# Other PSUM buffers and a new order for the first batch of an RWKV6 and mixer kernel, and a later place for one range flag

## The chip, the cores and the metric

The kernel runs on one core of a Trainium2 chip. The metric is the device time of one execution in microseconds (us). Of the kernel before there are three runs: 542.96, 543.42 and 543.53 us, with a median of 543.42 us.

A core has five engines that take their instructions in order, each from a queue of its own. TensorE (PE in the profile) multiplies matrices and writes the products to PSUM. VectorE (DVE) and ScalarE (ACT) do elementwise work and read PSUM. SyncE (SP) issues the transfers here, and GpSimd (POOL) has next to nothing to do. PSUM is held in banks of 512 float32 values on each of 128 partitions.

## The reference

There are two parts. The first is a linear attention with a decaying state, for 4 batches, 8 heads, 768 tokens and heads of 48:

```python
for t in range(S):
    cur = np.einsum('bhd,bhe->bhde', u[None] * kt, vt)
    y[:, :, t] = np.einsum('bhd,bhde->bhe', rt, state + cur)
    state = wt[:, :, :, None] * state + np.einsum('bhd,bhe->bhde', kt, vt)
```

The second takes x, which is y with heads and head sizes side by side (4 x 768 x 384), and mixes first over tokens, then over channels:

```python
h = np.maximum(xt @ w_tok1, 0.0) @ w_tok2      # xt: x with tokens last; 768 -> 256 -> 768
u = x + h.transpose(0, 2, 1)
h2 = np.maximum(u @ w_ch1, 0.0) @ w_ch2        # 384 -> 1536 -> 384
return (u + h2).astype(np.float32)
```

The four weights arrive as 64-bit floats. The kernel converts them to float32 itself.

## The kernel before, in words

**Attention by units.** A batch has 768 tokens. A unit is 256 of them, so a batch has three units and there are twelve in all (0 to 11). Within a unit the tokens form four chunks of 64. The loop over tokens of the reference becomes products over chunks, with the decays put into queries and keys. `unit(i)` returns the steps of unit i as functions:

- `ends` (L368) and `begins` (L376) are the running products of the decays (scans on VectorE), `keys` (L373) and `queries` (L379) multiply them into k and r.
- `tokens` (L281) transposes the keys on TensorE into two PSUM banks of the tag "m", and `copied` (L282) copies the two halves to SBUF on ScalarE.
- `carry` (L298) forms the products of keys and values per chunk, the state product `kv_ps`. `update` (L442, L444) adds the chunk's product to the scaled state on VectorE, and `scaled` (L434) scales the new state for the next chunk on ScalarE. So the two alternate: add, scale, add, scale.
- `own_gram` and `gram` (L251) are the products of keys and queries inside a chunk, the first with u. `own_put` (L391) and `mask` (L263, later L421) put them into the matrix `at` on VectorE.
- `before` (L313) multiplies the queries with the states into the PSUM tile of y, `after` (L334) adds the product of `at` and the values. Between them stands `seen` (L322 or L325), a small copy on ScalarE of y's last columns, called the view below. `taken` (L340) copies y to x in three parts.
- `ranges` (L360) are two passes on ScalarE over the decays, each leaving a flag of whether they are in range: `ranges[0]` the lower, `ranges[1]` the upper. The flags are summed near the end.

**PSUM in the first batch.** Three pools share it: `ps_a` with one buffer of two banks, `ps_g` with two buffers of two banks (tag "gram"), `ps_m` with two buffers of one bank (tag "m"). In units 0 to 2 the state product takes two banks of `ps_m`, which the transposed keys use also. y takes `ps_a` in units 0 and 1, and a buffer of `ps_g` in unit 2. After the first batch `ps_g` and `ps_m` make way for one pool of six single banks. From then on the state product takes `ps_a`, and grams, y and everything else single banks.

**Weights and mixing.** The weights are converted in pieces of 128 x 1024 values (`convert`). A piece is loaded, then has steps on VectorE and ScalarE in turn: exponent (L203), power of two (ScalarE, L206), mantissa (L209), sum (L215), signs (ScalarE, L212), product (L218, L221). Two raw buffers, `spare` and `scratch`, take turns; the next load into one waits for the conversion that reads it. The mixing of a batch runs a batch behind its attention: token mixing `hidden` (L515) and `back` (L522, with the add L524), transposes `turn` (L530), channel mixing `up` (L538, with L540 on ScalarE) and the second channel product, plain (L609) or in a form with seven products of quarters (L627, its first VectorE steps L637 and L668).

**Order.** For TensorE, VectorE and ScalarE `strict` fixes the order of issue as written: each instruction is issued after the one before it on its engine. The first batch is one list written out by hand (L718 to L726). In later batches `woven` merges the list of attention steps (`steps`, L687) with the list of mixing pieces by the weights that stand beside each entry, so that an entry's weight shifts what follows it. SyncE's transfers are not in that order; a scheduler places them.

Of the kernel before, what the change touches and what calls it, by code (L numbers as in the profile page):

```python
# [10 lines left out]
f32 = mybir.dt.float32  # L11
# [10 lines left out]
T = 64  # L22
# [40 lines left out]
def rwkv6_then_mixer(  # L63
# [46 lines left out]
    def bank(name):  # L110
        return ps_m.tile([128, 512], f32, name=name, tag="m")
# [175 lines left out]
            f()  # L287
        return kT

    def outer(kT, vt, half, apart=False):  # L290

        both = None if apart else ps_a.tile([128, 2, 512], f32, name="kv_ps", tag="a")
        kv = [bank("kv_ps") if apart else both[:, j] for j in range(2)]
        for c in range(UC):
            for a in range(A):
                for j, q in ((0, 0), (1, 1), (0, 1), (1, 0)):
                    if 2 * (half * UC + c) + j < 2 * C - 1:
                        pe.matmul(kv[j][ts(q, P), ds((c * A + a) * D, D)], kT[ts(j, T), c, a, ts(q, P)],  # L298
                                  vt[ts(j, T), c, ts(2 * a + q, D)], start=True, stop=True)
        return kv  # L300

    def across(r_, before, half, where=None):

        where = where or (ps_g and (ps_a, "a"))
        both = where and where[0].tile([128, 2, 512], f32, name="y_ps", tag=where[1])
        y = [both[:, q] for q in range(2)] if where else [bank("y_ps") for q in range(2)]
        begun = set()
        for c in range(UC):
            for a in range(A):
                for q, j in ((0, 0), (1, 0), (1, 1), (0, 1)):  # L310
                    g = 2 * (half * UC + c) + j
                    if g > 0:
                        pe.matmul(y[q][put(q, j), ds((c * A + a) * D, D)],  # L313
                                  r_[q * P:q * P + D, ds((c * A + a) * 128 + j * T, T)],
                                  before[g][q * P:q * P + D, a, :], start=(q, j) not in begun, stop=False,
                                  skip_group_check=True)
                        begun.add((q, j))

        def see():
            seen = apool.tile([128, 2], f32, name="seen")  # L320
            if where:
                act.copy(seen, both[:, :, X * D - 1])  # L322
            else:
                for q in range(2):
                    act.copy(seen[:, q:q + 1], y[q][:, X * D - 1:X * D])  # L325

        return y, see
# [14 lines left out]
    def unit(i):  # L342
# [78 lines left out]
                dve.tensor_mul(at[:, q], g, over_heads(strictly, g.shape[1]))  # L421

        def carry():
            L["kv"] = outer(L.pop("kT"), vs[i], half, apart=bt == 0)
# [11 lines left out]
        def update(c, j):  # L436
            g = 2 * (half * UC + c) + j
            if g < 2 * C - 1:
                new = state[bt, g + 1] = apool.tile([128, A, D], f32, name="state", bufs=3)
                got = L["kv"][j][:ROWS, ds(c * A * D, A * D)].rearrange("p (a e) -> p a e", a=A)  # L440
                if g == 0:
                    dve.tensor_copy(new[:ROWS], got)  # L442
                else:
                    dve.tensor_add(new[:ROWS], L["before"][g][:ROWS], got)  # L444

        def before():
            if half == 0:
                xs[bt] = xpool.tile([128, C, DM], f32, name="x")
            L["y"], L["see"] = across(r_, L["before"], half, (ps_g, "gram") if i == UB - 1 else None)

        def seen():
            L["see"]()
# [250 lines left out]

    hiddens, turned, ups, downs = mixing_of(0)
# [85 lines left out]
    def by_halves(b):  # L790
# [18 lines left out]
        for half in range(UB):  # L809
# [25 lines left out]
            for c in range(UC):  # L835
                for j in range(2):
                    g = 2 * (half * UC + c) + j
                    if g < 2 * C - 1:
                        new = states[g + 1] = apool.tile([128, A, D], f32, name="before", bufs=5)
                        got = kv[j][:ROWS, ds(c * A * D, A * D)].rearrange("p (a e) -> p a e", a=A)  # L840
# [54 lines left out]
```

## Time and profile before

The figures are of one profiled execution.

| what | value |
|---|---|
| median of the runs | 543.42 us |
| the profiled execution | 546.1 us |
| its span, first to last instruction | 544.3 us |
| mean granted TensorE clock | 0.971 |
| TensorE busy | 509.1 us, 94% |
| VectorE busy | 336.0 us, 62% |
| ScalarE busy | 212.6 us, 39% |

By stage (TensorE busy of the stage, and the clock granted in it):

| us from the start | TensorE busy | clock |
|---|---|---|
| 0 to 15 | 6.33 | 1.00 |
| 15 to 30 | 9.57 | 0.66 |
| 30 to 45 | 9.85 | 0.67 |
| 45 to 60 | 14.14 | 0.88 |
| 60 to 75 | 12.57 | 1.00 |
| 75 to 90 | 14.05 | 1.00 |
| 90 to 110 | 16.97 | 1.00 |
| 110 to 180 | 67.81 | 0.95 |
| 180 to 260 | 79.48 | 1.00 |
| 260 to 340 | 80.00 | 1.00 |
| 340 to 390 | 49.48 | 1.00 |
| 390 to 545 | 148.90 | 1.00 |

In the timeline a row gives the start, the length, the engine, the line, the operation, output <- inputs, the shape and the number of instructions. In brackets stand the idle time before it and what ended that. A wait is written as who waited <- for what: microseconds in total, times, longest. The matmuls of float32 appear as two records each. In the 40 slices of the span a digit is the busy share in tenths, or for PEclk the granted clock in tenths of full speed. Idle time of an engine that is not on the path that sets the end costs nothing.

### The profile page before, as it was taken

How to read it: one execution, taken by the hardware profiler on the slowest of the kernel's cores; microseconds unless marked ns; L12 is line 12 of the kernel's file. 1: busy time of each engine (PE TensorE's matmuls, PEld its weight loads, DVE VectorE, ACT ScalarE, POOL GpSimd, SP SyncE). 2: the span in 40 equal slices, each digit the busy share in tenths (PEclk: the TensorE clock that was granted, in tenths of full speed). 3: DMA queues.
4: the chain of work that ended last, by engine and by line, in shares of the span. 5: the costliest groups of instructions: out<-in, count | busy, mean ns of one | idle time of the engine just before them, and what ended most of it. 6: DMA issues, size and time to landing. Idle time of an engine off the chain costs nothing.

```text
span 544.3 us, 12657 instructions
## 1 busy us (share of the span) xinstructions
PE 509.1 (94%) x5542; PEld 439.9 (81%) x5542; DVE 336.0 (62%) x516; ACT 212.6 (39%) x534; POOL 1.3 (0%) x10
## 2 busy tenths in 40 slices
PE   3659979799899999999999999999999999999996
PEld 3548568676798967898998967898898977999996
DVE  7975999688672755175382655277294625775653
ACT  3856695753234323423324333423514313541400
POOL 0000000000000000000000000000000000000000
PEclk9677999989899999999999999999999999999999
DMA  8855747632321313104113112002000000000000
GB/s 310 327 147 161 251 136 238 208 107 62 97 88 53 108 55 117 40 31 145 41 60 107 51 59 98 30 4 88 1 27 5 2 30 1 1 1 31 1 32 32
DMA packets 20942, 46.01 MB, mean 85 GB/s; under 512 B 2128, under 2 KB 13008, under 8 KB 20880
## 3 DMA queue, kind: packets, MB, share of 16 engines
q1 hardware_dynamic: 20736, 45.14, 25.1%
q8 instruction: 45, 0.74, 0.6%
q14 instruction: 17, 0.14, 0.1%
q10 hardware_dynamic: 144, 0.00, 0.0%
HBM read 40.41 MB, written 4.72 MB: 83 GB/s over the span
## 4 chain that ended last, share of the span: by engine, by line
PE 79%; DVE 11%; ACT 4%; issue 3%; DMA 1%; DVEq 0%; ACTq 0%
PE q_ps L627 27%; PE z_ps L538 22%; PE z_ps L570 6%; PE h_ps L515 5%; PE h_ps L522 4%; PE h_ps L609 3%; PE y_ps L334 3%; PE gram L251 2%; PE kv_ps L298 2%; PE y_ps L313 2%; PE k_ps L281 2%; DVE to_end L368 1%; ACT scratch L212 1%; PE xT_ps L530 1%; DVE scratch L218 1%
## 5 line engine op out<-in xcount | busy, mean ns | idle before, releaser
L538 PE MATMUL z_ps<-xT,wch 128*128 128x256 f32 x648 | 148.9, 385 | 1.0 <-DVE wch L221 1.0
L538 PEld LDWEIGHTS z_ps<-xT,wch 128*128 128x128 f32 x648 | 121.8, 192 | 18.1 <-DVE wch L221 1.4
L627 PE MATMUL q_ps<-wch,z 128*128 128x192 f32 x492 | 87.0, 328 | 0.0
L627 PEld LDWEIGHTS q_ps<-wch,z 128*128 128x128 f32 x492 | 80.4, 190 | 1.3 <-DVE z L669 0.3
L540 ACT ACTIVATE z<-z_ps 128x256 f32<-128x256 f32 x108 | 40.7, 382 | 83.7 <-PE z_ps L538 83.1
L627 PE MATMUL q_ps<-scratch,z 128*128 128x192 f32 x324 | 58.2, 334 | 2.2 <-DVE z L668 2.2
L434 ACT ACTIVATE before<-state,to_end 112x48 f32<-112x48 f32 x176 | 44.2, 323 | 34.4 <-DVE state L444 31.7
L627 PEld LDWEIGHTS q_ps<-scratch,z 128*128 128x128 f32 x324 | 54.6, 195 | 2.7 <-DVE z L668 2.5
L444 DVE TENSOR_TENSOR state<-before,kv_ps 112x192 f32<-112x192 f32 x40 | 14.0, 350 | 44.8 <-ACT before L434 31.4
L522 PE MATMUL h_ps<-h,wtok 128*128 128x384 f32 x96 | 35.2, 492 | 0.6 <-ACT h L517 0.6
L637 DVE TENSOR_TENSOR o<-x,z 128x192 f32<-128x192 f32 x8 | 2.9, 358 | 50.9 <-ACT z L636 46.4
L515 PE MATMUL h_ps<-x,wtok 128*128 128x384 f32 x96 | 32.6, 495 | 0.0
L524 DVE TENSOR_TENSOR x<-x,h_ps 128x384 f32<-128x384 f32 x24 | 13.3, 552 | 27.4 <-PE h_ps L522 27.2
L368 DVE TENSOR_TENSOR_SCAN to_end<-w,starts 112x1041 f32<-112x1041 f32 (+1 forms) x13 | 28.1, 2160 | 2.1 <-DMA w<-in_w_dram 1.7
L376 DVE TENSOR_TENSOR_SCAN w<-w,starts 112x1041 f32<-112x1041 f32 x12 | 27.8, 2320 | 0.0
L515 PEld LDWEIGHTS h_ps<-x,wtok 128*128 128x128 f32 x96 | 18.3, 194 | 11.8 <-issue 0.5
L360 ACT ACTIVATE junk<-to_end,least 112x1041 uint8<-112x1041 f32 x12 | 13.9, 1162 | 28.3 <-DVE to_end L368 28.3
L522 PEld LDWEIGHTS h_ps<-h,wtok 128*128 128x128 f32 x96 | 16.6, 190 | 10.1 <-ACT h L517 2.8
L340 ACT COPY x<-y_ps 64x384 f32<-64x384 f32 (+1 forms) x36 | 17.1, 476 | 18.1 <-PE y_ps L334 17.7
L281 PE MATMUL k_ps<-ident,rk 128*128 128x128 f32 x96 | 15.4, 311 | 6.2 <-issue 4.4
L334 PEld LDWEIGHTS y_ps<-vt,at 64*64 64x64 f32 x768 | 14.5, 148 | 7.3 <-ACT seen L325 4.6
L334 PE MATMUL y_ps<-vt,at 64*64 64x48 f32 x768 | 16.0, 234 | 4.6 <-ACT seen L325 3.3
(140 smaller groups left out, 672.8 us busy)
## 6 DMA issues: line engine op xcount, KB each, us to landing
rk<-in_rk_dram SPq DMA_DIRECT2D x36, 192.0 KB, 3.6
near<-in_near_dram SPq DMA_DIRECT2D x8, 768.0 KB, 4.3
w<-in_w_dram SPq DMA_DIRECT2D x11, 520.5 KB, 3.3
spare<-in_w_ch_dram SPq DMA_DIRECT2D x10, 512.0 KB, 4.5
vt<-in_v_dram SPq DMA_DIRECT2D x12, 384.0 KB, 4.2
out_dram<-o SPq DMA_DIRECT2D x24, 192.0 KB, 1.9
scratch<-in_w_ch_dram SPq DMA_DIRECT2D x8, 512.0 KB, 4.2
rk<-in_rk_dram SPq DMA_DIRECT2D x6, 512.0 KB, 8.6
```

Of the source, the lines that this page charges most:

```text
L281: pe.transpose(both[c][:, a, :], k_[:, ts(c * A + a, 128)], ident)
L334: pe.matmul(y[q][put(q, j), ts(ca, D)], at[ts(j, T), q, ca, :], vt[ts(j, T), c, ts(2 * a + q, D)], start=False, stop=ca == 0, skip_group_c ...
L340: return [lambda: act.copy(x[:, 0], got[0])] + [lambda n=n: act.copy(x[ts(n, P), 1], got[1][ts(1 - n, P)]) for n in range(2)]
L368: dve.tensor_tensor_scan(to, of, start, 0.0, op0=ALU.mult, op1=ALU.add)
L376: dve.tensor_tensor_scan(w_[:ROWS], w_[:ROWS], starts[:ROWS], 0.0, op0=ALU.mult, op1=ALU.add)
L434: act.mul(t[:ROWS, a], state[bt, g][:ROWS, a], by_last(c, j)[:, a:a + 1])
L515: pe.matmul(sums[i], wtok1[:, c, ts(i, 128)], x_of()[:, c, :], start=(c == 0), stop=(c == C - 1))
L522: pe.matmul(ps, wtok2[:, i, ts(c, 128)], h1[:, i, :], start=(i == 0), stop=(i == DTOK // 128 - 1))
L538: pe.matmul(ps, wch1[:, m, ts(jt, 128)], xT[:, m, ts(s, SEG)], start=(m == 0), stop=(m == DM // 128 - 1))
L540: act.activation(zs[s][:, jt, :], ps, AF.Relu)
L570: pe.matmul(ps[:, q], lefts[r][:, ts(q, 128)], of[r], start=first and q == 0, stop=end and q == JB - 1, skip_group_check=True)
L627: pe.matmul(ps, a[:, j, :], b[:, j, :], start=(j == 0), stop=(j == HJ - 1))
```

## The change

There are three edits.

1. In the first batch the state product takes `ps_a`, the buffer that only it uses from now on, and y takes a buffer of the tag "gram" in all three units. The transposed keys and the first mixing products have the two banks of `ps_m` to themselves. `outer` loses its argument `apart`, and `across` its argument `where`.
2. The hand-written order of the first batch is set anew, to match. Unit 1's `own_put` stands ahead of its `carry` and `gram`; unit 2's `keys` and `tokens` stand after the first update of unit 1, with `own_gram` and `carry` later; unit 2's `own_put` and `gram` stand after unit 1's `after`, and only two instead of four of the `hidden` products precede unit 2's y.
3. In units 3 to 11 `ranges[1]` moves from ahead of the last update to the place between `seen` and `after`, and its weight in the weaving is 1.5 instead of 0.4. Since the list of a batch is woven by its total weight, other pieces shift by a place or two too.

```diff
-    def outer(kT, vt, half, apart=False):
-        both = None if apart else ps_a.tile([128, 2, 512], f32, name="kv_ps", tag="a")
-        kv = [bank("kv_ps") if apart else both[:, j] for j in range(2)]
+    def outer(kT, vt, half):
+        kv = ps_a.tile([128, 2, 512], f32, name="kv_ps", tag="a")
...
-    def across(r_, before, half, where=None):
-        where = where or (ps_g and (ps_a, "a"))
-        both = where and where[0].tile([128, 2, 512], f32, name="y_ps", tag=where[1])
-        y = [both[:, q] for q in range(2)] if where else [bank("y_ps") for q in range(2)]
+    def across(r_, before, half):
+        both = ps_g and ps_g.tile([128, 2, 512], f32, name="y_ps", tag="gram")
+        y = [both[:, q] for q in range(2)] if ps_g else [bank("y_ps") for q in range(2)]
...
-            L["y"], L["see"] = across(r_, L["before"], half, (ps_g, "gram") if i == UB - 1 else None)
+            L["y"], L["see"] = across(r_, L["before"], half)
...
-                *([(1.3, e["sums_put"])] if by_tokens else []), (0.4, e["ranges"][1]), (0.7, up[3]),
-                (0.1, lambda: load_w(i + 2)), (1.0, e["before"]), (0.1, e["seen"]), (1.0, e["after"]), *some(e["taken"], 0.3),
+                *([(1.3, e["sums_put"])] if by_tokens else []), (0.7, up[3]),
+                (0.1, lambda: load_w(i + 2)), (1.0, e["before"]), (0.1, e["seen"]), (1.5, e["ranges"][1]), (1.0, e["after"]), *some(e["taken"], 0.3),
...
-           e1["keys"], e0["after"], *e2["own_u"], e1["tokens"], *e1["copied"], e1["queries"], e1["carry"], *e0["taken"], lambda: load_v(2),
-           e1["gram"], e2["ends"], e2["keys"], s1[0], t1[1], e2["tokens"], e1["own_put"], e2["own_gram"], s1[1], t1[2], *e2["copied"],
-           e2["begins"], e2["carry"], s1[2], t1[3], e1["mask"], s1[3], t2[0], e1["before"], e2["queries"], e2["gram"], s2[0], t2[1], e1["seen"],
-           e1["after"], x1, m1, s2[1], t2[2], e1["taken"][0], *h[:4], e2["own_put"], s2[2], t2[3], e1["taken"][1], p1, e2["mask"], e1["taken"][2],
-           s2[3], e2["before"], e2["seen"], add1, g1, put1, to_ch[0][0], e2["after"], *h[4:8], x2, m2, *e2["taken"], p2, add2, g2, *h[8:], put2,
+           e1["keys"], e0["after"], *e2["own_u"], e1["tokens"], *e1["copied"], e1["queries"], e1["own_put"], e1["carry"], *e0["taken"],
+           lambda: load_v(2), e1["gram"], e2["ends"], s1[0], t1[1], e2["keys"], e2["tokens"], s1[1], t1[2], e2["own_gram"], *e2["copied"],
+           e2["begins"], s1[2], t1[3], e1["mask"], s1[3], t2[0], e2["carry"], e1["before"], e2["queries"], s2[0], t2[1], e1["seen"],
+           e1["after"], e2["own_put"], e2["gram"], s2[1], t2[2], x1, e1["taken"][0], m1, *h[:2], s2[2], t2[3], e1["taken"][1], p1, e2["mask"],
+           e1["taken"][2], s2[3], e2["before"], e2["seen"], add1, g1, put1, to_ch[0][0], e2["after"], *h[2:8], x2, m2, *e2["taken"], p2,
+           add2, g2, *h[8:], put2,
```

Here e0, e1, e2 are the units 0 to 2, s1 and t1 the updates and scalings of unit 1, h the `hidden` products, and x, m, p, add, g, put with a number the steps of that weight conversion: exponent, mantissa, power, sum, signs, product.

More of the change, by code (lines that the diff above doesn't have):

```diff
@@ L297, in outer @@
                     if 2 * (half * UC + c) + j < 2 * C - 1:
-                        pe.matmul(kv[j][ts(q, P), ds((c * A + a) * D, D)], kT[ts(j, T), c, a, ts(q, P)],
+                        pe.matmul(kv[ts(q, P), j, ds((c * A + a) * D, D)], kT[ts(j, T), c, a, ts(q, P)],
                                   vt[ts(j, T), c, ts(2 * a + q, D)], start=True, stop=True)
         return kv
-    def across(r_, before, half, where=None):
-        where = where or (ps_g and (ps_a, "a"))
-        both = where and where[0].tile([128, 2, 512], f32, name="y_ps", tag=where[1])
-        y = [both[:, q] for q in range(2)] if where else [bank("y_ps") for q in range(2)]
+    def across(r_, before, half):
+        both = ps_g and ps_g.tile([128, 2, 512], f32, name="y_ps", tag="gram")
+        y = [both[:, q] for q in range(2)] if ps_g else [bank("y_ps") for q in range(2)]
         begun = set()
@@ L320, in see @@
             seen = apool.tile([128, 2], f32, name="seen")
-            if where:
+            if both is not None:
                 act.copy(seen, both[:, :, X * D - 1])
@@ L423, in carry @@
         def carry():
-            L["kv"] = outer(L.pop("kT"), vs[i], half, apart=bt == 0)
+            L["kv"] = outer(L.pop("kT"), vs[i], half)
         def by_last(c, j):
@@ L439, in update @@
                 new = state[bt, g + 1] = apool.tile([128, A, D], f32, name="state", bufs=3)
-                got = L["kv"][j][:ROWS, ds(c * A * D, A * D)].rearrange("p (a e) -> p a e", a=A)
+                got = L["kv"][:ROWS, j, ds(c * A * D, A * D)].rearrange("p (a e) -> p a e", a=A)
                 if g == 0:
@@ L839, in by_halves @@
                         new = states[g + 1] = apool.tile([128, A, D], f32, name="before", bufs=5)
-                        got = kv[j][:ROWS, ds(c * A * D, A * D)].rearrange("p (a e) -> p a e", a=A)
+                        got = kv[:ROWS, j, ds(c * A * D, A * D)].rearrange("p (a e) -> p a e", a=A)
                         if g == 0:
```

## The prediction

> **What bounds the kernel now.** First the page: busy shares and the 40 slices.
>
> ```profile
> PE 509.1 (94%) x5542; PEld 439.9 (81%) x5542; DVE 336.0 (62%) x516; ACT 212.6 (39%) x534; POOL 1.3 (0%) x10
> PE   3659979799899999999999999999999999999996
> DVE  7975999688672755175382655277294625775653
> PEclk9677999989899999999999999999999999999999
> ```
>
> TensorE is full from slice 9 (110 us) on; its idle time lies in the first batch, at a low clock. There only a removed wait or better clock can shorten the span; later, only what stops TensorE. Next, TensorE's waits:
>
> ```profile
> PE k_ps L281 <- issue: 4.4, 1, 4.4
> PE y_ps L334 <- ACT seen L325: 3.3, 4, 1.9
> PE y_ps L313 <- ACT before L434: 2.3, 2, 1.2
> PE q_ps L627 <- DVE z L668: 2.2, 1, 2.2
> ```
>
> "issue" names no releaser, so I put the timelines beside it, TensorE first, then VectorE and ScalarE:
>
> ```profile
> 35.56 1.08 PE L281 MATMUL k_ps<-ident,rk 128*128 128x128 f32 x4 [4.42 <-issue]
> 37.37 1.12 PE L281 MATMUL k_ps<-ident,rk 128*128 128x128 f32 x4 [0.73 <-ACT kT L282]
> 40.18 1.92 PE L298 MATMUL kv_ps<-vt,kT 64*64 64x48 f32 x44
> 53.32 5.43 PE L515 MATMUL h_ps<-x,wtok 128*128 128x384 f32 x16
> ...
> 35.13 0.33 DVE L444 TENSOR_TENSOR state<-before,kv_ps 112x192 f32<-112x192 f32 x1
> 40.05 0.35 DVE L444 TENSOR_TENSOR state<-before,kv_ps 112x192 f32<-112x192 f32 x1 [3.38 <-ACT before L434]
> 53.30 0.69 DVE L218 TENSOR_TENSOR scratch<-scratch 128x1024 bf16<-128x1024 bf16 x1 [4.76 <-ACT scratch L212]
> ...
> 39.01 1.01 ACT L434 ACTIVATE before<-state,to_end 112x48 f32<-112x48 f32 x4
> 52.12 1.15 ACT L212 ACTIVATE scratch<-spare 128x1024 bf16<-128x1024 int32 x1
> ```
>
> Unit 2's key transposes start 0.1 us after unit 1's third state add: they wait for a bank that unit 1's state product holds. Only one is free, so the second half waits for the first half's copy. Unit 1's last scaling (39.01) stands behind those copies on ScalarE, so the last add waits 3.38, and unit 2's state product starts at 40.18. From there TensorE runs to 58.75 with 0.28 idle. Unit 2's y view precedes the signs L212, and VectorE waits 4.76 for those. From 53.3 to 109 VectorE's conversions and TensorE lean on each other; the chain of waits runs through both.
>
> **What the Trainium skill says.** "PSUM — Partial Sum Buffer", Specifications: eight banks of 2 KiB per partition. Pools of two, two times two and two use all of them, so products can only trade places; the stall above agrees. "TensorE: Matmul & The Clock Gate", Architectural detail: ScalarE and VectorE are strict FIFO; the 3.38 us agree. The same page, Part 1: a clock gate looks at free-running windows of 3413 ns, half rate after an idle window. The means over 2 us stretches (0.99 at 16:18, 0.95 at 28:30, 0.75 at 34:36, 0.83 at 48:50, 0.50 between the pairs) put the changes at 18.0, 28.2, 35.0 and 48.7: gaps of 3, 2 and 4 windows, which agrees. But 64-row matmuls filling 41.8 to 45.2 did not lift it here, and a window with 1.5 us of them busy (14.6 to 18.0) lost it.
>
> **The change as a whole.** It adds and removes no work: the same matmuls, copies and transfers stand in another order and in other banks, as the changed program's order on each engine shows. So each term below is a wait that goes, comes or moves, in the times of the trace before.
>
> **Step 1, unit 2's transposes.** With state products in their own pair, both key banks are free at 29.0 (unit 1's copies). The transposes now wait for VectorE's L373 of unit 2. own_put of unit 1 (1.22; 1.16 start to start) moves ahead of unit 2's scan, because unit 1's gram now needs that buffer: scan 28.7, reciprocal 31.1, first add 31.3, keys 31.5 to 32.7. Transposes at 32.75 instead of 35.56, and the 0.73 goes. The gram of unit 1 is not delayed: own_put ends at 28.7, the gram started at 29.92.
>
> **Step 2, unit 2's state product.** Unit 1's second scaling ends at 34.05, the copies at 35.05, the scan L376 at 35.2, third add 35.15 to 35.5, last scaling 35.55 to 36.55, last add to 37.0. Product at 37.05 instead of 40.18: 3.1 gained.
>
> **Step 3, TensorE to the end of h.** The work from there is the same (18.3 busy), reordered; h gives 2 matmuls before unit 2's y instead of 4. New stops: 0.1 at unit 1's view, about 0.4 where unit 2's y waits, 0.1 at its view. That y takes the buffer of unit 1's y, so it waits for that one's last copy, behind two scalings, two copies and L206 (42.05 + 0.45 + 1.0 + 0.45 + 1.15 + 0.45 = 45.6 at best, 46.8 at low clock); before, it began at 50.81. At equal clock 3.1 - 0.6 = 2.5. Clock: in place of 4.4 idle there are 1.7 and 2.0, so the low stretch (35.0 to 48.7) starts a window later or ends one earlier, or neither: 0 to 1.7 us, since 64-row matmuls take 1.7 times as long there (L334: 1.96 for 64 at 24.5, 1.15 at 52.2). I take 0.8. **Together 3.3; bounds 2.0 and 4.5.**
>
> **Step 4, VectorE.** Signs L212 start at 47 to 49 instead of 52.12: 3.3 to 5.2 gained, more than TensorE. But the x adds L524 stand in VectorE's order, and the first (60.99) came as it was free and data was ready; so VectorE is held to TensorE's 3.3. The first channel-weight load is issued after those signs (53.29) and used at 60.26; both move together. On SP, v for unit 3 and half of unit 1's successor loads change places; unit 3's first scan is at 74.25, so nothing waits. I carry 3.3 to 100 us.
>
> **Step 5, unit 3's flag.**
>
> ```profile
> 105.16 1.15 ACT L360 ACTIVATE junk<-to_end,most 112x1041 uint8<-112x1041 f32 x1
> 107.61 1.09 ACT L212 ACTIVATE scratch<-spare 128x1024 bf16<-128x1024 int32 x1
> 108.87 0.20 ACT L325 COPY seen<-y_ps 128x1 f32<-128x1 f32 x2
> ```
>
> The view leaves this queue ahead of the flag and of L212, needing only y (105.6) and L206: ready near 106.5, and six more z matmuls stand before its user. The 1.95 goes. Against it, y itself comes three z matmuls (six of the trace's records, 1.3 us) earlier, and waits longer for its last scaling: 1.8 against 1.08, so 0.7 back. Sum about 1.3; bounds 0.6 and 2.0. The flag (1.15 + 0.19) now precedes the copies of y and some z copies, which have banks to spare.
>
> **Step 6, unit 4.** After the first stores VectorE waits 4.48 for a store, then L668 releases q (TensorE idle 2.2, and half clock after: 12 records in 3.86 instead of 2.1). Now y stands ahead of q, and needs the last scaling, which follows the gram mask (1.28), L668 (0.96) and an add: up to 2.9 after the store lands, against 1.3 to q. But the sums L401 come 1.35 earlier, so the 768 KB near load runs ahead of that store, which I let land 1.3 earlier (142.8 to 141.5). y's end then lies near 145.4: between 1.9 gained, if the clock holds, and 1.4 lost, if the store lands as before. I take 0.8.
>
> **Step 7, units 6, 9, 10.** The view waits 0.52, 0.52, 0.28 go: 1.3. In units 5 and 11 y comes one or two products sooner, beside its last scaling: 0.3 back. 1.0.
>
> **Sum.** 3.3 + 1.3 + 0.8 + 1.0 = 6.4. The profiled execution took 546.1 (span 544.3, 1.8 around it): 539.7 for one like it. The median of the runs is 543.42, 2.7 lower; waits are the same in kind, so 543.4 - 6.4 = **537.0**.
>
> **Rivals.** *The first batch gives half:* the clock stays low until the longer run of h at 50 us, or conversions, not TensorE, set the pace after 70, where VectorE is busy 14.8 of the 15 us from 75. Step 3 gives 1.2 and unit 4 loses 0.5: 543.4 - 1.2 - 1.3 + 0.5 - 1.0 = 540.4. For it: 64-row work did not lift the clock. Against: 3.4 us of TensorE waits between 67 and 80 can absorb lag. *No gain at all:* the removed 4.4 is replaced, wait for wait, by keys, last add and buffer; later queues move nothing: 543.2. Against: steps 1 and 2 use shown durations. *Slower:* the buffer wait of unit 2's y takes the place of the bank wait. Every us beyond 50.8 goes one to one into L212 and the conversions; with 3.1 from steps 5 to 7 the kernel is slower once that y starts after 54. At 56: 543.4 + 5.2 - 3.1 = 545.5. For it: ScalarE has scalings, copies and L206 ahead of the release. Against: that queue sums to 46.8 even at low clock.
>
> **Numbers.** As worked out 0.55 (own range 534.8 to 539.3), half 0.26, none 0.08, slower 0.11. No change is within 0.2%, 1.1 us. The 80% range is 534.6 to 541.6: most of the two faster cases, leaving out the last two. Faster 0.81, same 0.08, slower 0.11.
>
> **What would show it.** Right: the transposes start near 32.8 after L373, no 4.4 "issue"; unit 2's state product near 37; L212 before unit 2's copies at 47 to 49; VectorE's 4.76 shrunk to about 2; unit 3's view wait gone, its scaling wait near 1.8; no view waits later. Wrong: unit 2's y after 50, a low clock past 50, TensorE idle over 3 us near unit 4's y, or VectorE waits for weight loads around 60.

## The result, and the profile after

| what | before | after |
|---|---|---|
| median of the runs, us | 543.78 (542.96 to 546.6) | 539.57 (538.26 to 540.50) |
| ratio after : before | | 0.9915, 95% interval 0.9887 to 0.9943 |
| profiled execution, us | 546.1 | 538.77 |
| its span, us | 544.3 | 537.1 |
| mean granted TensorE clock | 0.971 | 0.978 |

The change makes the kernel faster by 4.6 us as the ratio has it, with an interval of 3.1 to 6.1 us. In a second set, with other kernels beside it, the same program took 538.93 us (ratio 0.9909, 0.9886 to 0.9932; row e9 below). Forecast were 537.0 us and a gain of 6.4. The two profiled executions differ by 7.3 us, more than the medians do, because the profiled execution of before is one of its longer ones (546.1 in a range up to 546.6). That difference matters below. In the changed program the line numbers from 300 on are 2 lower: L334 of before is L332, L515 is L513, L637 is L635.

TensorE's waits after (who <- for what: total us, times, longest):

```profile
PE y_ps L311 <- ACT before L432: 5.5, 3, 2.2
...
PE kv_ps L297 <- DVE state L442: 2.0, 1, 2.0
PE k_ps L281 <- issue: 1.8, 2, 1.5
```

The 4.4 of "issue" ahead of the transposes is gone (1.8 in two), the view waits of later units (L323 after, L325 before) and the wait of q for L666 (L668 before) don't appear any more. In their place stand 5.5 us for the scaling L432, in three waits of up to 2.2 (2.3 us in two before), and 2.0 for an add of the state.

The timeline after (start, length, engine, line, operation, output <- inputs, and in brackets the idle time and what ended it); first TensorE, then VectorE, then ScalarE, then the issues of SyncE's queue:

```profile
33.20 1.06 PE L281 MATMUL k_ps<-ident,rk 128*128 128x128 f32 x8 [1.52 <-issue]
...
37.37 1.07 PE L297 MATMUL kv_ps<-vt,kT 64*64 64x48 f32 x45 [2.02 <-DVE state L442]
...
46.17 1.15 PE L311 MATMUL y_ps<-before,rk 48*64 48x48 f32 x64
...
101.15 0.99 PE L311 MATMUL y_ps<-before,rk 48*64 48x48 f32 x28 [2.17 <-ACT before L432]
...
105.94 5.45 PE L536 MATMUL z_ps<-xT,wch 128*128 128x256 f32 x24
...
139.19 0.99 PE L311 MATMUL y_ps<-before,rk 48*64 48x48 f32 x28 [1.88 <-ACT before L432]
140.11 5.85 PE L625 MATMUL q_ps<-scratch,z 128*128 128x192 f32 x24
...
146.97 4.17 PE L625 MATMUL q_ps<-wch,z 128*128 128x192 f32 x24
...
31.88 1.21 DVE L371 TENSOR_TENSOR rk<-rk,to_end 112x1024 f32<-112x1024 f32 x1
...
36.97 0.35 DVE L442 TENSOR_TENSOR state<-before,kv_ps 112x192 f32<-112x192 f32 x1
...
48.64 0.69 DVE L218 TENSOR_TENSOR scratch<-scratch 128x1024 bf16<-128x1024 bf16 x1 [2.21 <-ACT scratch L212]
...
136.08 0.36 DVE L635 TENSOR_TENSOR o<-x,z 128x192 f32<-128x192 f32 x1 [3.17 <-DMA out_dram<-o]
...
47.47 1.13 ACT L212 ACTIVATE scratch<-spare 128x1024 bf16<-128x1024 int32 x1
...
130.94 0.35 SPq L151 DMA_DIRECT2D near<-in_near_dram  x1
132.67 0.34 SPq L612 DMA_DIRECT2D out_dram<-o  x1
```

In the first batch the transposes start 0.1 us after unit 2's keys L371 (31.88 + 1.21), the state product 2.8 us earlier than before, unit 2's y at 46.17 instead of 50.81, and VectorE's wait for the signs L212 is 2.21 instead of 4.76. The end of h, the last L513, is at 55.39 instead of 58.75.

From unit 3 on, the flag no longer stands ahead of the views. But the scaling waits there are 2.17 us (101.15) and 1.88 us (139.19). The second is behind a wait of VectorE for a store (L635, 3.17), and after it TensorE runs at half clock for a while: 24 records of q take 5.85 us (140.11), where 24 take 4.17 at full clock (146.97 in the same trace).

### The profile page after: what moved, and what is told of

Same layout as the page of the kernel before. It is cut to its first block, busy times and chain, and to the rows that moved or that the text cites. A ratio compares the mean times of both kernels' runs of the same rounds, so it can differ in the third digit from the quotient of the medians.

```text
span 537.1 us, 12655 instructions
## 1 busy us (share of the span) xinstructions
PE 506.5 (94%) x5542; PEld 437.7 (82%) x5542; DVE 336.7 (63%) x516; ACT 212.8 (40%) x534; POOL 1.3 (0%) x10
## 4 chain that ended last, share of the span: by engine, by line
PE 81%; DVE 9%; DMA 4%; ACT 3%; issue 2%; SPq 1%; DVEq 0%
PE q_ps L625 28%; PE z_ps L536 23%; PE h_ps L513 6%; PE z_ps L568 6%; PE h_ps L520 5%; PE h_ps L607 3%; PE y_ps L332 2%; PE y_ps L311 2%; DMA w<-in_w_dram 2%; PE gram L251 2%; PE kv_ps L297 2%; DMA rk<-in_rk_dram 2%; PE k_ps L281 1%; PE xT_ps L528 1%; DVE wch L221 1%
## 5 line engine op out<-in xcount | busy, mean ns | idle before, releaser
L432 ACT ACTIVATE before<-state,to_end 112x48 f32<-112x48 f32 x176 | 44.2, 323 | 34.4 <-DVE state L442 31.3
L635 DVE TENSOR_TENSOR o<-x,z 128x192 f32<-128x192 f32 x8 | 2.9, 358 | 49.8 <-ACT z L634 46.6
L513 PE MATMUL h_ps<-x,wtok 128*128 128x384 f32 x96 | 32.8, 497 | 0.0
L513 PEld LDWEIGHTS h_ps<-x,wtok 128*128 128x128 f32 x96 | 18.4, 195 | 11.9 <-issue 0.6
L311 PEld LDWEIGHTS y_ps<-before,rk 48*64 48x64 f32 x704 | 14.6, 143 | 9.0 <-ACT before L432 6.1
L311 PE MATMUL y_ps<-before,rk 48*64 48x48 f32 x704 | 16.6, 232 | 5.5 <-ACT before L432 5.5
L529 ACT COPY xT<-xT_ps 128x384 f32<-128x384 f32 x24 | 11.4, 478 | 23.9 <-PE xT_ps L528 23.8
```

What stands on the lines that cost most here:

```text
L311: pe.matmul(y[q][put(q, j), ds((c * A + a) * D, D)], r_[q * P:q * P + D, ds((c * A + a) * 128 + j * T, T)], before[g][q * P:q * P + D, a, ...
L432: act.mul(t[:ROWS, a], state[bt, g][:ROWS, a], by_last(c, j)[:, a:a + 1])
L513: pe.matmul(sums[i], wtok1[:, c, ts(i, 128)], x_of()[:, c, :], start=(c == 0), stop=(c == C - 1))
```

## The experiments

Each kernel is the changed one with an edit, unless the text says that it is the kernel before. The times are medians in us, with their range. Ratios are to runs of the kernel before in the same set, whose medians were 544.34 for e1 to e4, 543.95 for e5 to e8 and 544.56 for e9 to e12; so ratios are what is compared between sets.

| run | kernel | median (range) | ratio (95% interval) |
|---|---|---|---|
| e1 | first batch only, flag as before | 539.91 (538.97 to 541.16) | 0.9919 (0.9895 to 0.9942) |
| e2 | before, with the flag's edit only | 541.83 (540.37 to 545.00) | 0.9956 (0.9940 to 0.9972) |
| e3 | changed, flag's weight 0.4 | 538.54 (537.51 to 539.49) | 0.9891 (0.9867 to 0.9914) |
| e4 | before, with the new banks only | 543.19 (542.13 to 545.19) | 0.9979 (0.9968 to 0.9990) |
| e5 | changed, near load after the store | 536.77 (535.25 to 537.30) | 0.9870 (0.9842 to 0.9898) |
| e6 | e3 and e5 together | 535.49 (535.04 to 535.55) | 0.9841 (0.9818 to 0.9864) |
| e7 | e3, sums of z ahead of the store's wait | 536.10 (535.48 to 536.42) | 0.9851 (0.9823 to 0.9878) |
| e8 | changed, four full-array matmuls added | 540.45 (538.64 to 542.14) | 0.9933 (0.9907 to 0.9959) |
| e9 | changed, again | 538.93 (538.13 to 541.34) | 0.9909 (0.9886 to 0.9932) |
| e10 | before, near load after the store | 541.45 (540.79 to 543.36) | 0.9947 (0.9927 to 0.9966) |
| e11 | e1, near load after the store | 538.14 (536.52 to 539.39) | 0.9883 (0.9862 to 0.9904) |
| e12 | e6, two full-array matmuls added | 534.62 (533.38 to 535.91) | 0.9822 (0.9800 to 0.9844) |

For single traces I use four marks on TensorE: the end of the token products h in the first batch; the start of the q products that follow unit 4's y (short: q4); the start of the last batch's h; and the end. From the last of these marks to the end the traces take 104.6 to 104.7 us, but e4 and e5 only 103.7 and 103.6; that difference lies behind the last product.

| trace | end of h | q4 | q4 to last h |
|---|---|---|---|
| before | 58.75 | 152.38 | 287.23 |
| after, and again in e9 | 55.39, 55.93 | 146.97, 147.02 | 285.45, 285.44 |
| e1 first batch only | 54.10 | 145.71 | 287.22 |
| e2 flag only | 57.97 | 149.05 | 285.44 |
| e3 weight 0.4 | 55.32 | 145.40 | 286.39 |
| e4 new banks only | 59.71 | 150.20 | 287.22 |
| e5 near load later | 54.94 | 144.42 | 285.45 |
| e6 both | 55.27 | 142.77 | 286.39 |
| e7 sums of z first | 55.33 | 143.90 | 286.15 |
| e8 four matmuls added | 56.30 | 148.33 | 285.44 |
| e10 before, near load later | 58.49 | 147.98 | 287.23 |
| e11 first batch, near load later | 56.89 | 144.37 | 287.22 |
| e12 e6 with two matmuls | 54.54 | 140.59 | 286.39 |

### Which part of the change brings it (e1, e2, e4)

e1 takes the flag's edit out:

```diff
-                *([(1.3, e["sums_put"])] if by_tokens else []), (0.7, up[3]),
-                (0.1, lambda: load_w(i + 2)), (1.0, e["before"]), (0.1, e["seen"]), (1.5, e["ranges"][1]), (1.0, e["after"]), *some(e["taken"], 0.3),
+                *([(1.3, e["sums_put"])] if by_tokens else []), (0.4, e["ranges"][1]), (0.7, up[3]),
+                (0.1, lambda: load_w(i + 2)), (1.0, e["before"]), (0.1, e["seen"]), (1.0, e["after"]), *some(e["taken"], 0.3),
```

> Edits 1 and 2 alone (new buffers and order of the first batch; the upper flag and its weight as before). My theory: steps 1 to 4 hold by themselves, so this is faster than before by 3.3 us (2.0 to 4.5), unit 2's transposes start near 33 and its state product near 37, and the waits for unit 3's view (about 2 us) and of the later units' views (0.5, 0.5, 0.3) stay. Rival (first batch gives half, clock or conversions set the pace): 1.2 us or less.

e2 is the kernel before with that edit alone.

> Edit 3 alone on the kernel before (upper flag behind the view, weight 1.5). My theory: steps 5 to 7 hold by themselves, faster by about 3 us (1.5 to 4): unit 3's view wait gone, its wait for the last scaling up to about 2, no later view waits, and unit 4's y waits for its last scaling in place of the product that waited for L668. Rival (the later queue moves little, since what the view no longer waits for is waited for elsewhere): 1 us or less.

e4 has the new banks (edit 1) with the order of before, but for unit 1's `own_put`, which stands ahead of its `carry` and `gram`, since the gram now needs that buffer:

```diff
-           e1["keys"], e0["after"], *e2["own_u"], e1["tokens"], *e1["copied"], e1["queries"], e1["carry"], *e0["taken"], lambda: load_v(2),
-           e1["gram"], e2["ends"], e2["keys"], s1[0], t1[1], e2["tokens"], e1["own_put"], e2["own_gram"], s1[1], t1[2], *e2["copied"],
+           e1["keys"], e0["after"], *e2["own_u"], e1["tokens"], *e1["copied"], e1["queries"], e1["own_put"], e1["carry"], *e0["taken"], lambda: load_v(2),
+           e1["gram"], e2["ends"], e2["keys"], s1[0], t1[1], e2["tokens"], e2["own_gram"], s1[1], t1[2], *e2["copied"],
```

> The buffers of edit 1 with the old order of the first batch, but for unit 1's own_put ahead of its state product (its gram needs that buffer), and the flag as before. My theory: the transposes start at once after the keys (near 32.5), but unit 2's gram now needs the buffer that its own_put frees late, and it stands ahead of unit 1's second part of y; so TensorE stalls about 2 us there and the gain is 1 to 2 us. If the banks alone were the cause (rival), the gain is that of the first batch as a whole, about 3.3.

The first batch alone gives 4.4 us (0.0081 of 544.34), the flag alone 2.4 (0.0044). Together they would be 6.8, but the whole change gives 4.6 to 5.0 by its two ratios: beside the new first batch the flag's edit is worth 0.2 to 0.5 us by the ratios, far less than the width of their intervals, and e1 and the changed kernel can't be told apart. Both parts by themselves came out inside the theories written above, and both rivals (1.2 us or less, 1 us or less) fell; what no theory had is that the two don't add up.

The banks alone give 1.1 us. TensorE in e4, timeline:

```profile
38.44 1.83 PE L297 MATMUL kv_ps<-vt,kT 64*64 64x48 f32 x45 [3.40 <-DVE state L442]
...
43.97 1.99 PE L251 MATMUL gram<-rk 48*64 48x64 f32 x64 [1.87 <-DVE at L389]
...
51.73 1.15 PE L311 MATMUL y_ps<-before,rk 48*64 48x48 f32 x64
```

The transposes start at 32.88, as early as in the changed kernel, but the state product then waits 3.40 us for the last add of unit 1 (unit 2's keys L371 still stand ahead of unit 1's first add, so that the last add comes at 38.04 instead of 36.97), unit 2's gram waits for its buffer until VectorE's L389 has read it, and y starts at 51.73, later than before. So the banks only take the first wait away; the order of VectorE's and TensorE's work had to follow. By the traces even the 1.1 us don't come from the first batch: in e4 h ends at 59.71, 1.0 later than before, and the gain comes behind it, where units 3 and 4 of e4 lose nothing to half clock and those of before lose 1.6 us twice. What the banks alone are worth stays open.

e1's trace shows what the flag's edit meets beside the new first batch. TensorE, then VectorE:

```profile
100.47 2.42 PE L536 MATMUL z_ps<-xT,wch 128*128 128x256 f32 x6
103.98 2.06 PE L332 MATMUL y_ps<-vt,at 64*64 64x48 f32 x64 [1.09 <-ACT seen L323]
...
139.19 2.22 PE L625 MATMUL q_ps<-scratch,z 128*128 128x192 f32 x12 [2.10 <-DVE z L666]
...
137.79 0.36 DVE L635 TENSOR_TENSOR o<-x,z 128x192 f32<-128x192 f32 x1 [4.38 <-DMA out_dram<-o]
```

At unit 3 the two waits of e1 are 1.07 and 1.09 us, 2.16 together, where the changed kernel has one of 2.17. The second is short only because the six records of z before it ran at half clock (2.42 us instead of 1.56). At unit 4 q waits 2.10 for the sum L666, and the changed kernel waits 1.88 for a scaling instead. So in these two traces the edit moves both waits to another instruction and removes neither. At q4 the changed kernel is even 1.3 us later (146.97 and 147.02 against 145.71), but its h had ended 1.3 to 1.8 later: from the end of h to q4 the changed kernel takes 91.58 and 91.09 (e9), e1 91.61. Each runs at half clock in one place on the way, e1 at unit 3 and the changed kernel at unit 4 (e1's 12 records of q take 2.22, at full clock). Behind q4 the edit gives 1.78 us, in every pair of traces to 0.01.

### The weight of the flag (e3)

```diff
-                (0.1, lambda: load_w(i + 2)), (1.0, e["before"]), (0.1, e["seen"]), (1.5, e["ranges"][1]), (1.0, e["after"]), *some(e["taken"], 0.3),
+                (0.1, lambda: load_w(i + 2)), (1.0, e["before"]), (0.1, e["seen"]), (0.4, e["ranges"][1]), (1.0, e["after"]), *some(e["taken"], 0.3),
```

> The changed kernel with the flag's weight back at 0.4: the flag stands behind the view, but the weaving is as before, so unit 3's y has three z matmuls before its view's user and unit 4's y stands behind one product again. My theory: unit 3's wait for its last scaling falls from 2.2 to about 1.1 with no wait for the view, unit 4 has the product's wait for the store (about 2) again; together within 0.8 us of the changed kernel. If the weight is what carries the gain (rival), this is slower than the changed kernel by 1.5 us or more.

The new place needs the weight only for what it shifts: with 0.4, y isn't moved ahead of other products as far. In the trace unit 3 waits 1.07 for the scaling and 0.55 for the view, and up to q4 it is 1.6 us ahead of the changed kernel; behind q4 it has 0.94 less of the gain, of which about 0.5 is one more view wait that is left there. By the ratios it is 1.0 to 1.3 us faster than the changed kernel, where I had expected 0.8 at most and no view wait. The intervals overlap, so by itself the weight isn't settled. Its trace pointed to the next question. VectorE, then TensorE:

```profile
135.92 0.36 DVE L635 TENSOR_TENSOR o<-x,z 128x192 f32<-128x192 f32 x1 [4.42 <-DMA out_dram<-o]
...
137.33 3.77 PE L625 MATMUL q_ps<-scratch,z 128*128 128x192 f32 x12 [2.14 <-DVE z L666]
```

VectorE waits 4.42 us for a store before L635, q waits 2.14 for the sum L666 behind it, and q then runs at half clock (12 records in 3.77). In before it is the same pair: 4.48 and 2.2.

### The store that everything at unit 4 waits for (e5, e6, e10, e11, e7)

The output tile `o` has one buffer. So L635, the first step of a new pair of output rows, waits until the store of the pair before it has landed. And unit 5's near load of 768 KB is issued ahead of the second of those stores. The edit places it behind:

```diff
-                (0.7, up[0]), (0.3, by[1]), (1.4, e["gram"]), (1.0, sums[2]), (0.1, lambda: load_near(i + 1)),
+                (0.7, up[0]), (0.3, by[1]), (1.4, e["gram"]), (1.0, sums[2]), *([] if i == 4 else [(0.1, lambda: load_near(i + 1))]),
...
-                (0.1, lambda: load_w(i + 2)), (1.0, e["before"]), (0.1, e["seen"]), (1.5, e["ranges"][1]), (1.0, e["after"]), *some(e["taken"], 0.3),
+                *([(0.1, lambda: load_near(i + 1))] if i == 4 else []), (0.1, lambda: load_w(i + 2)), (1.0, e["before"]), (0.1, e["seen"]), (1.5, e["ranges"][1]), (1.0, e["after"]), *some(e["taken"], 0.3),
```

The load also gets a dependency on the store L612, so that it is issued after it. TensorE's order is the same with and without the edit; on VectorE one later mask step (L404) moves by one place, behind the state add on which unit 4's y waits.

> The changed kernel, with unit 5's near load (768 KB) issued after the second store of unit 4's time instead of ahead of it; all else is as in the changed kernel. Theory: unit 4's state adds and output add stand on VectorE behind L635, which waits for that store, and the store is slow because the near load is ahead of it on SP's queue. Then the store lands about 1 us sooner (2.3 instead of 3.3 us), L635 starts near 135.1 instead of 136.1, unit 4's y waits 0.9 instead of 1.9 us for its scaling, and the time falls by 0.8 to 1.5 us from the changed kernel's 539.6. Rival: a store of 192 KB takes 3 us to land whatever is ahead of it; the wait and the time stay.

> The changed kernel with the flag's weight 0.4 in its new place, and unit 5's near load after the second store. With weight 0.4 alone q waited 2.14 us for the sum of L666, behind L635's wait of 4.42 us for the store, and half clock followed (538.5 us). Theory: the store lands some 2 us sooner, the wait of q and the half clock behind it go, and the time is 536 to 537. Rival: the wait goes, but the time comes back at the view or scaling wait that follows; 538.5.

> The kernel before, with unit 5's near load issued after the second store of unit 4's time, and nothing of the change. Theory: the wait for the store is older than the change (VectorE waits 4.48 us for it in the trace of before, and TensorE stands still for about 2 us and runs at half clock behind that), and so it is worth about 2.5 us there too: 541 to 542.5. Rival: only the change brought the wait onto TensorE's path; 543.5 to 544.5.

> The first batch's part of the change with the flag as before, and unit 5's near load after the second store. The first batch alone gave 539.9 with a wait of 2.1 us of q for the sum of L666. Theory: the flag's part is worth 1.3 to 2.4 us where the store isn't late, so this gives 537.5 to 538.5, against 536.8 for the whole change with the near load later. Rival: the flag's part is worth nothing beside the first batch's; then 536.8.

e5's timeline, VectorE, TensorE and SyncE's queue:

```profile
135.22 0.36 DVE L635 TENSOR_TENSOR o<-x,z 128x192 f32<-128x192 f32 x1 [1.79 <-DMA out_dram<-o]
...
138.32 0.99 PE L311 MATMUL y_ps<-before,rk 48*64 48x48 f32 x28 [0.49 <-ACT before L432]
139.25 4.17 PE L625 MATMUL q_ps<-scratch,z 128*128 128x192 f32 x24
...
130.60 2.95 SPq L612 DMA_DIRECT2D out_dram<-o  x2
133.60 0.42 SPq L151 DMA_DIRECT2D near<-in_near_dram  x1
```

VectorE's wait for the store, in the traces: 4.38 to 4.67 us where the near load is issued 0.46 us ahead of it (before, e1, e3, e4), 2.99 to 3.33 where it is 1.73 ahead (e2, after, e8, e9), and 1.79 to 1.81 where it comes behind (e5, e6, e10, e11, e12). TensorE's wait at unit 4 shrinks from 1.88 to 0.49 in e5, and goes altogether in e6 and e10, with the half clock behind it. The time falls by 3.1 us in the kernel before (e10, by the medians; the others are by the ratios), by 2.0 in the first batch's part (0.9919 to 0.9883), by 2.1 to 2.4 in the changed kernel (0.9915 and 0.9909 to 0.9870) and by 2.7 with weight 0.4 (0.9891 to 0.9841). So the wait is older than the change, and the theory of e5 holds in all four. In e5 and e6 the gain is larger than expected (0.8 to 1.5 for e5); e5's estimate left out the half clock behind the wait. The Trainium skill, "DMA: Bandwidth & Descriptors", Queues, rings and completion order, says that on each DMA engine a queue's descriptors (the pieces of its transfers) are consumed in the order of the ring; the later landing of a store with a large load ahead of it agrees. The two stores of e5 land 2.0 us after their issue (median).

With the store early the first batch's part gives 3.3 us (541.45 to 538.14, one set). The flag's edit on top of it gives 0.7 by the ratios (0.9883 to 0.9870) and 1.4 by the medians, and with weight 0.4 it gives 2.3 and 2.65. The 1.3 to 2.4 us of e11's theory are met at weight 0.4, not clearly at 1.5.

e7 leaves the store late, and takes out of its shadow what doesn't need the tile:

```diff
-            return [(1.96, p1), (0.01, lambda: dve.tensor_add(s1, a21, a22)), (1.96, p4),
-                    (0.01, lambda: dve.tensor_sub(s2, s1, a11)), (1.96, p2), (0.01, lambda: dve.tensor_sub(a21, a11, a21)),
+            return [(0.01, lambda: dve.tensor_add(s1, a21, a22)), (0.01, lambda: dve.tensor_sub(s2, s1, a11)), (1.96, p1),
+                    (1.96, p4), (1.96, p2), (0.01, lambda: dve.tensor_sub(a21, a11, a21)),
```

> The changed kernel with the flag's weight 0.4, and in each quarter of the second layer the two sums of z that don't need the output buffer (L666 and the first of L667) put ahead of the first product and its output add L635. The store and the near load stay in their order. Theory: q no longer waits for the store through L666; the wait of 2.14 us goes while L635 waits as long as before; 536.5 to 537.5, a part of the gain being taken by unit 4's state adds, which still stand behind L635, so that its y waits for the scaling for up to 1 us. Rival: the state adds set the end anyway; 538.5.

```profile
137.25 0.36 DVE L635 TENSOR_TENSOR o<-x,z 128x192 f32<-128x192 f32 x1 [2.99 <-DMA out_dram<-o]
...
139.75 0.99 PE L311 MATMUL y_ps<-before,rk 48*64 48x48 f32 x28 [0.65 <-ACT before L432]
```

VectorE still waits 2.99 for the store, and gets to L635 as late as 137.25; q runs without a wait, and y waits 0.65 for its scaling, as the state add stands behind the store. The kernel gains 2.2 us (0.9891 to 0.9851), nearly what the earlier store gives; each of its four runs is shorter than all six of e3. So it isn't the store's time by itself that counts, but what stands behind it on VectorE.

### The granted clock in the first batch (e8, e12)

In the changed kernel's trace the clock is low from about 38.7 to 45.5. The stretches of 2 us of the changed kernel (busy time and instructions of PE, PEld, DVE, ACT and POOL; then the clock, the share of the DMA engines and GB/s):

```profile
38.00:40.00 2.00, 1.97 (x84) 1.81 (x78) 1.72 (x3) 1.21 (x6) 0.00 (x0) 0.67 0.31 66
40.00:42.00 2.00, 1.74 (x64) 1.74 (x68) 2.00 (x5) 1.22 (x6) 0.00 (x0) 0.50 0.87 290
42.00:44.00 2.00, 2.00 (x74) 1.88 (x69) 0.04 (x1) 1.70 (x6) 0.00 (x0) 0.50 0.64 166
```

The edit adds matmuls ahead of unit 2's own gram, into the buffer that this gram then writes over; four of them in e8, and two, on top of e6, in e12:

```diff
-    def grams(k_, r_):
+    def grams(k_, r_, full=None):
...
-        g = [both[:, q] for q in range(2)] if ps_g else [bank("gram") for q in range(2)]
+        g = [both[:, q] for q in range(2)] if ps_g else [bank("gram") for q in range(2)]; [pe.matmul(both[:, 0], ident, full[:, :512], start=True, stop=True) for _ in range(4 if full is not None else 0)]
...
-            L["own"] = grams(L.pop("uk"), r_)
+            L["own"] = grams(L.pop("uk"), r_, k_ if i == 2 else None)
```

> The changed kernel with four full-array matmuls (128 rows, 512 columns, their output is written over) added ahead of unit 2's own gram, in the 2 us in which TensorE waits for unit 1's last state add. They cost about 2.1 us of TensorE's time in an idle stretch of 2.0. Theory: they keep the granted clock at full from 38 to 45, where the changed kernel's trace has 0.5; unit 2's y starts near 45 instead of 46.2, and the time falls by about 1 us to 538.5. Rival: the clock drops all the same, in this or another stretch, or the fill delays the state product; 539.6 to 540.5.

> Weight 0.4 and the near load later (535.5), with two full-array matmuls of 128 rows by 512 columns (output written over) ahead of unit 2's own gram. Four of them took 3.6 us and made the state product 1.4 us late; two take 1.8 us, within the 2.0 us in which TensorE waits. Theory: the granted clock stays at full from 36 to 45, unit 2's y starts near 45 instead of 46, and the time is 534.3 to 535.0. Rival: the low stretch costs nothing, or moves elsewhere: 535.5.

In both some of SyncE's loads of r and k are issued in another order too; TensorE waits for no transfer because of it.

e12's stretches:

```profile
38.00:40.00 2.00, 1.47 (x87) 1.34 (x79) 1.30 (x3) 0.90 (x4) 0.00 (x0) 1.00 0.48 131
40.00:42.00 2.00, 1.59 (x91) 1.47 (x95) 2.00 (x5) 1.32 (x7) 0.00 (x0) 1.00 0.67 240
42.00:44.00 2.00, 2.00 (x55) 1.29 (x45) 1.28 (x3) 1.99 (x7) 0.00 (x0) 1.00 0.43 112
```

Both kept the full clock from 34 to 50. I had mis-estimated the size: the four take 3.60 us, not 2.1, so that in e8 the state product starts at 38.78 instead of 37.37 and unit 2's y at 47.07, and nothing is gained: the rival of e8, that the fill delays the state product, came true. The two of e12 take 1.88 and fit: y starts at 45.31 instead of 46.04 in e6, h ends 0.7 earlier, and the median is 0.9 lower. Four of its five runs lie below all five of e6, but the intervals of the ratios overlap, so the gain is likely rather than shown. e1 and e5 had a low stretch too, but a short one, at 32.8 to 36.3, where TensorE was waiting anyway, and their h ended at 54.10 and 54.94: the cost depends on where the stretch falls. None of the eight traces with the new first batch and no fill is without a low stretch there.

e12 is the fastest of all, 9.7 us (1.8%) below the kernel before and 4.7 to 5.1 below the changed one by the ratios.

### The changed kernel again (e9)

> The changed kernel as it is, for comparison within this set. Expected 539.6 (538.3 to 540.5) as before; with weight 0.4 it was 538.5 and with the near load after the store 536.8, so that this run says how much of these differences is the day's.

538.93, with a trace that repeats the first one's to within 0.1 us at q4. The differences of 2 us and more above are not the day's.

## Why the prediction was right, and where its sum was not

The forecast of 537.0 us lies 1.9 to 2.6 us below the two medians; the sign was right, and so was the first batch as the largest part. Both medians lie inside the range given, 534.6 to 541.6; the first, 539.57, lies just outside the narrower 534.8 to 539.3 of the case as worked out. By the traces the parts are 3.0 to the end of h, nothing at units 3 and 4, and 1.8 behind them: 4.8, beside a measured 4.6 and 5.0 and a forecast 6.4. That the total came so near is in part luck, since the last part came out 0.8 above its forecast, half of it for a reason that was not traced, against the 2.1 that failed to come.

**Steps 1 and 2 (transposes and state product)**: forecast 32.75 and 37.05, found 33.20 and 37.37 (33.58 and 37.75 in e9). The named releasers are those found: L371 and unit 1's last add. The 0.73 wait went.

**Step 3 (to the end of h)**: forecast 3.3, bounds 2.0 and 4.5. Three traces with the old first batch (before, e2, e10) end h at 57.97 to 58.75, eight with the new one (without e4 and the fills of e8 and e12) at 54.10 to 56.89. The means, 58.40 and 55.40, differ by 3.0. The low stretch is shorter, 6.8 us (38.7 to 45.5) instead of 13.7 (35.0 to 48.7). The 0.8 us for the clock was a mean over things that do happen: the stretch costs about 1 us where it falls on the dense work (after) and nothing where it falls on a wait (e1). The fill of e12 shows the size again. The median of e1 gains more than these 3.0, namely 4.4. In the traces the rest lies behind h, where the order is that of before (93.63 us to q4 in before, 91.61 in e1), and half clock accounts for most of it at units 3 and 4: twice in before, once in e1. How much of that is in the medians, single traces don't say.

**Step 4 (VectorE)**: signs at 47.47 (forecast 47 to 49), VectorE's wait 2.21 (about 2). No wait for weights came at 60 us.

**Steps 5 and 6 (units 3 and 4) are where the sum failed.** I had 1.3 and 0.8 us. Beside the new first batch they gave next to nothing: from the end of h to q4 91.61 us without the flag's edit (e1), 91.58 and 91.09 with it. The mechanisms are as written: the view wait of unit 3 is gone, the scaling wait grew, to 2.17 instead of the forecast 1.8; the sums come earlier, so the near load leaves earlier and the store lands 1.3 us earlier; and y waits for the last scaling behind mask, L666 and an add. What I mis-sized is what the earlier store is worth to TensorE: y needs an instruction that stands later on VectorE than the one that q needed, so TensorE waits as long as before (1.88 against 2.19), only for something else. And I put the half clock that follows into the old order only; it follows in the new one as well (5.85 for 4.17). With the store early e11, without the flag's edit, takes 87.48 from the end of h to q4. e5, with it, takes 89.48, but loses 1.7 of that to half clock at unit 3 (12 records of z in 4.54, where the changed kernel takes 2.86 behind the same wait), and e6, at weight 0.4, takes 87.50. So there too the traces show no gain of the two steps, at either weight; closer than the half clock of one stall they don't settle it.

**Step 7 (later units)**: forecast 1.0, found 1.78 from q4 to the last h, in every pair at weight 1.5. The view waits of 1.3 went; the 0.3 that I took back was not there. Where the other 0.5 comes from I did not trace.

**The baseline.** I took the profiled execution to stand 2.7 us above the median with the same waits. The waits were the same in kind, but its half clock need not be part of every execution: behind unit 3's view wait its 24 records of z take 7.02 us instead of 5.45, behind q's wait its 12 take 3.86 instead of 2.22. e1, with the same order there, has half clock at one of these places, e4 and e11 at neither. So the traces of before and after differ by 7.3, and the medians by 4.2 to 5.6. How many executions of before have both I can't say from the one trace of it.

**The rivals.** "The first batch gives half" named 540.4 and comes nearest to the measured time, but for the wrong reason: the first batch gave its 3 us, and units 3 and 4 didn't give theirs. The buffer wait of unit 2's y, the slower rival, did not come: y started at 46.17, long before 54. e4 shows how near it was: with the old order it started at 51.73.

## What to carry to other kernels

When a reordering puts another consumer first in line behind a late producer, the stall is not gone: follow the new first consumer down its own engine's queue, and compare the place of the instruction that it needs with the place of the old one. Ask of every wait that survives such a change what the producer itself is late for; here it was a small store behind a large load on one queue, and moving the load was worth as much as half of the change. When two edits are forecast apart, cost the second in the frame that the first one leaves, not in the trace of before.

## What the runs showed of the hardware that was not expected

- A stall of about 2 us on TensorE was followed by half clock in some traces and not in others. At unit 4 it cost 1.5 to 1.7 us in before, after, e9 and e3, and nothing in e1 (2.10 us of waiting). At unit 3 a wait of 2.0 to 2.2 us cost 1.6 to 1.7 in e2, e5 and e8, and nothing in the changed kernel and e9.
- What decides in the main is how the stall falls on a grid in time. In each of the 14 traces, up to about 150 us, every low stretch starts and ends on one grid of windows of 3.41 us and fills whole windows of it (after: 38.7 to 45.5 and 141.1 to 144.5, 30 windows from start to start). From 20 us on half clock followed each of the 19 windows at full clock in which TensorE was busy for 1.6 us or less, 7 of the 48 with 1.6 to 2.4 us, and none of the others. (The start is left out: the record shows full clock there, but 64 records of the gram take 1.99 us at 8.67 in before, and 1.16 at 82.19.) e5's stall at unit 3 (98.02 to 100.07) lies inside the window from 97.75 to 101.16, which has 1.36 us of work; that of the changed kernel (98.98 to 101.15) is shared by two windows, with 2.25 and 2.40, and costs nothing. The Trainium skill, "TensorE: Matmul & The Clock Gate", Part 1, has free-running windows of 3.4 us, and the traces agree; but it speaks of an idle window, and here a window that was half idle was enough.
- 3.60 us of 128-row matmuls in the wait (e8), or 1.88 (e12), kept the clock at full through the 64-row and 48-row matmuls that followed. Without them these ran at half clock in six of eight traces, and in the other two (e1, e5) the low stretch had come just before. In e6 the window from 34.81 to 38.22 has 1.39 us of work and half clock follows, in e12 the one from 34.90 to 38.32 has 2.90 and none follows. The matmuls that fill 41.8 to 45.2 in before without lifting the clock, and which the prediction calls 64-row, are nearly all of 48 rows (L313 and L251).
- A store of 192 KB with a 768 KB load issued 0.46 us ahead of it on the same queue kept VectorE 2.6 to 2.9 us longer than with the load behind it (4.38 to 4.67 against 1.79 to 1.81).
